# A two-layer attention and MLP kernel: value products on four column tiles, TensorE repack of late outputs, additions shared with GpSimd

## Chip, cores, metric

One core of one Trainium2 chip. The metric is the device time of one launch in microseconds; lower is better. Before: 1644.31 us, median of 3 runs (1643.47 to 1644.97).

## The reference, cut to what matters

Sequence 2048, width 512, two identical layers, each an attention part (A) and a gated MLP part (B):

```python
def _A_ref(x, wq, wk, wv, wo):            # H = 32 heads of 16, one shared K and V head
    q = (x @ wq) -> heads; k = x @ wk; v = x @ wv
    p = softmax(einsum("bhqd,bkd->bhqk", q, k) * 16 ** -0.5)
    return concat_heads(p @ v) @ wo
def _B_ref(x, w1, w2, w3, w4):
    h = gelu(layernorm(x) @ w1); hs = shift_rows(h) @ w2      # rows shifted by 1, -1, 2, -2
    x1 = x + hs
    return x1 + gelu(layernorm(x1) @ w3) @ w4
x = x + A(ln(x)); x = x + B(ln(x)); x = x + A(ln(x)); x = x + B(ln(x))
```

The scores make 32 x 2048 x 2048 exponentials a layer. That is the bulk of the work.

## The kernel before

The program is written by a planner that runs when the kernel is built: every operation is declared with its inputs, an assumed duration and a priority; the planner simulates the engines, decides in which order each engine issues its instructions, and that order is then fixed. Engines work strictly in that order and wait on semaphores.

Attention is cut into 2048 **half-groups** of two heads by 512 scores. Most take the ScalarE way: one exponential of 128 x 1024 values, then one product with V. The others take the VectorE way: two conversions to integers J that read as bf16 powers of two, two additions JK of constants, and three products with V scaled by three weights.

```python
# one half-group on VectorE (cut)
for i in range(2):                                   # two J from PSUM
    o = op("DVE", ... tensor_scalar(J[i], in0=PB[bank], 128*LOG2E*0.25, 127*128, mult, add) ...)
for k in (1, 2):                                     # two JK, from J
    self.adds = [p for p in self.adds if not p.placed]
    eng = "POOL" if len(self.adds) < self.ADDS else "DVE"          # ADDS = 0: always VectorE
    x = op(eng, ... tensor_scalar(JK[r], in0=J, STEPS[k], 1.0, add, mult) ...)

# product with V: head h owns column tile h; half-group p owns two of the four tiles (cut)
for i in range(2):
    h = 2 * p + i
    e.matmul(PB[32*h:32*h+32, ACC, 0:w], lhsT=v[:, la, kb+j, :], rhs=ap[:, i, j*w:(j+1)*w],
             tile_position=(0, 32*h), ...)

# end of a block of four heads: normalise, then move 16 rows a head into OT (cut)
op("SP", lambda e: [e.dma_start(OT[r0+16*h : r0+16*h+16, b//2, 0:n], OS[32*h : 32*h+16, m, 0:n])
                    for h in range(4)], parts=4, prio=5)
```

TensorE also runs fillers, products of zeros that the planner puts in so that TensorE's clock isn't lowered. The MLP of one chunk runs beside the attention of the next. Between the layers lies a **passage**: layer 2 can start on the first tiles, but most of its keys need the end of layer 1. After the last exponential comes the **tail**: what is left of the MLP.

The softmax here doesn't subtract the row's maximum and nothing guards it: scores larger than these inputs give would overflow.

## Time and profile before

| | before |
|---|---|
| time, median (range) | 1644.31 us (1643.47 to 1644.97) |
| span of the profiled run | 1641.6 us |
| ScalarE busy / idle | 1535.7 / 105.9 us |
| exponentials on ScalarE | 1545 of 2048 half-groups |
| ScalarE idle, 770 to 950 us | 29.0 us |
| from the last exponential to the end | 59.0 us |

A busy share alone does not tell whether a shorter busy part would shorten the span. The lines are in the prediction. Two stretches of the time-ordered view of before, start and duration first (us): a value product that stands alone, and the end of the last attention block.

```profile
801.60 0.39 PE L1075 MATMUL PB<-JK,VD 128*32 128x512 bf16 x2
...
1593.51 0.41 DVE L1135 TENSOR_TENSOR OS<-ACCF,PB 128x256 bf16<-128x256 bf16 x1
1593.95 2.41 SPq L1140 DMA_DIRECT2D OT<-OS  x4
...
1597.60 1.91 PE L607 MATMUL PB<-WO,OT 128*32 128x512 bf16 x32 [1.07 <-DMA OT<-OS]
```

Two matmuls, two of four column tiles, where a run of four takes no longer.

### The profile page before, as it was taken

To read this page: it belongs to the slowest core of one execution; us is meant where nothing else is said; L and a number is where in the kernel's file an instruction comes from. 1 tells how busy PE (TensorE), PEld (TensorE's weight loads), DVE (VectorE), ACT (ScalarE), POOL (GpSimd) and SP (SyncE) were. 2 spreads that over 40 slices of the span, in tenths; PEclk is the share of its full clock that TensorE was granted. 3 is DMA by queue.
4 is the path that set the end of the run, shared out by engine and by line. 5 is a ranking of instruction groups with operands and counts; after the bars stand their busy time and mean duration, and the time that the engine had idled before them with its cause. 6 is when DMAs were issued, how large, how long until landed. Compare 5 with 4: busy or idle time off the path is not lost.

```text
span 1641.6 us, 47631 instructions
## 1 busy us (share of the span) xinstructions
PE 1617.8 (99%) x21141; PEld 545.5 (33%) x21141; DVE 1414.8 (86%) x2978; ACT 1535.7 (94%) x1623; POOL 105.6 (6%) x162
## 2 busy tenths in 40 slices
PE   8999999999999999999999999999999999999999
PEld 3222223322332223233333332333223223444454
DVE  8999999889999789898986798998899987899853
ACT  4999999999999999999797999999999999999952
POOL 3000000000010001100120000010000000010001
PEclk9999999999999999999999999999999999999999
DMA  6000000000100000100000000000000000000000
GB/s 204 17 4 4 5 18 5 5 3 5 18 5 3 5 3 5 18 5 5 2 2 2 2 8 8 5 18 4 14 11 4 4 5 11 19 5 5 6 17 18
DMA packets 24398, 20.79 MB, mean 13 GB/s; under 512 B 7168, under 2 KB 23680, under 8 KB 24192
## 3 DMA queue, kind: packets, MB, share of 16 engines
q1 hardware_dynamic: 24192, 17.75, 4.1%
q8 instruction: 165, 2.70, 0.7%
q14 instruction: 41, 0.34, 0.1%
HBM read 7.90 MB, written 2.10 MB: 6 GB/s over the span
## 4 chain that ended last, share of the span: by engine, by line
ACT 75%; PE 22%; DVE 2%; DMA 0%; POOL 0%; issue 0%; SPq 0%; POOLq 0%
ACT EA L997 70%; PE PB L607 10%; PE PB L953 6%; PE PB L1075 5%; ACT G L1364 2%; ACT L997 1%; ACT GP L1288 1%; ACT L1288 1%; PE PB L773 1%; ACT L1364 0%; DVE ST L713 0%; DVE G L1357 0%; DVE ZR L756 0%; DMA X<-in_A_x_dram 0%; POOL X L1371 0%; DVE J L1018 0%
## 5 line engine op out<-in xcount | busy, mean ns | idle before, releaser
L997 ACT ACTIVATE EA<-PB 128x1024 bf16<-128x1024 f32 x1545 | 1423.2, 1084 | 58.4 <-PE PB L1075 34.1
L1018 DVE TENSOR_SCALAR J<-PB 128x512 uint16<-128x512 f32 x1006 | 651.0, 683 | 107.5 <-PE PB L953 103.4
L953 PE MATMUL PB<-QT,KT 32*128 32x512 bf16 (+1 forms) x4608 | 623.3, 360 | 9.9 <-ACT EA L997 7.1
L1075 PE MATMUL PB<-EA,VP 128*32 128x512 bf16 (+1 forms) x3482 | 465.6, 362 | 0.9 <-DVE ACCF L1107 0.3
L1028 DVE TENSOR_SCALAR JK<-J 128x1024 uint16<-128x1024 uint16 x1006 | 387.5, 427 | 13.6 <-PE PB L1075 7.6
L953 PEld LDWEIGHTS PB<-QT,KT 32*128 32x128 bf16 x4608 | 159.9, 91 | 565.8 <-ACT EA L997 506.0
L1075 PE MATMUL PB<-JK,VD 128*32 128x512 bf16 (+1 forms) x2252 | 331.8, 361 | 0.2
L1075 PE MATMUL PB<-J,VD 128*32 128x512 bf16 (+1 forms) x1126 | 186.4, 361 | 2.6 <-DVE J L1018 2.6
L607 PE MATMUL PB<-ZT,W 128*32 128x512 bf16 (+2 forms) x2816 | 170.8, 344 | 0.5 <-DVE J L1018 0.4
L1075 PEld LDWEIGHTS PB<-EA,VP 128*32 128x32 bf16 x3482 | 121.3, 94 | 137.7 <-issue 114.6
L607 PE MATMUL PB<-ONES,NIL 128*32 128x512 bf16 x1416 | 143.7, 392 | 4.5 <-DVE ZR L756 1.3
L1075 PEld LDWEIGHTS PB<-JK,VD 128*32 128x32 bf16 x2252 | 90.5, 95 | 107.2 <-issue 54.7
L607 PE MATMUL PB<-W,G 128*32 128x512 bf16 x1792 | 125.2, 382 | 0.3 <-ACT G L1353 0.2
L730 POOL TENSOR_SCALAR SM<-MV 128x4 f32<-128x4 f32 (+3 forms) x30 | 9.6, 319 | 1137.6 <-DVE MV L715 1137.6
L1357 DVE CAST G<-PB 128x512 bf16<-128x512 f32 (+2 forms) x126 | 72.9, 582 | 10.1 <-PE PB L607 8.5
L607 PEld LDWEIGHTS PB<-ZT,W 128*32 128x32 bf16 x2816 | 57.4, 96 | 56.0 <-issue 33.4
L1075 PEld LDWEIGHTS PB<-J,VD 128*32 128x32 bf16 x1126 | 51.0, 95 | 36.1 <-issue 20.1
L1135 DVE TENSOR_TENSOR OS<-ACCF,PB 128x512 bf16<-128x512 bf16 (+1 forms) x72 | 44.7, 621 | 12.6 <-PE PB L1129 8.1
L1364 ACT ACTIVATE G<-G 128x3584 bf16<-128x3584 bf16 (+2 forms) x18 | 46.0, 2601 | 9.8 <-DVE G L1357 9.7
L607 PEld LDWEIGHTS PB<-W,G 128*32 128x32 bf16 x1792 | 37.5, 95 | 46.9 <-issue 26.8
L607 PEld LDWEIGHTS PB<-ONES,NIL 128*32 128x32 bf16 x1416 | 36.0, 96 | 38.5 <-issue 8.0
L1371 POOL TENSOR_TENSOR X<-Y,X 128x512 f32<-128x512 bf16 x32 | 38.4, 1204 | 154.4 <-DVE Y L1326 149.6
(83 smaller groups left out, 824.5 us busy)
## 6 DMA issues: line engine op xcount, KB each, us to landing
W<-in_B_w_dram SPq DMA_DIRECT2D x2, 1792.0 KB, 15.2
OT<-OS SPq DMA_DIRECT2D x224, 16.0 KB, 1.8
QT<-QS SPq DMA_DIRECT2D x40, 64.0 KB, 2.4
X<-in_A_x_dram SPq DMA_DIRECT2D x8, 256.0 KB, 5.2
out_dram<-OUTB SPq DMA_DIRECT2D x16, 128.0 KB, 1.7
W<-in_B_w_dram SPq DMA_DIRECT2D x2, 512.0 KB, 9.0
OT<-OS SPq DMA_DIRECT2D x64, 8.0 KB, 1.8
WQ<-in_A_wq_dram SPq DMA_DIRECT2D x1, 512.0 KB, 4.9
```

The lines of the kernel that those rows point to most:

```text
L607: ins = e.matmul(self.PB[32 * g:32 * g + 32, bank, 0:n], lhsT=lhsT[:, 32 * g:32 * g + 32], rhs=rhs, start=start, stop=stop, tile_position= ...
L773: ins = e.transpose(self.PBH[:, L.bank, j * 512 + i * 128:j * 512 + (i + 1) * 128], self.ZR[:, tb % 4, dc * 128:(dc + 1) * 128], self.IDENT)
L953: ins = e.matmul(self.PB[:, bank, j * n:(j + 1) * n], lhsT=self.KT[32 * h:32 * h + 32, la, (kb + j) * 128:(kb + j + 1) * 128], rhs=self.QT ...
L997: o = q.feeds = op("ACT", lambda e: e.activation(self.EA[:, ea, :, :], self.PB[:, b0:b0 + 2, :], ACTF.Exp, scale=0.25), writes=bk + [("EA" ...
L1018: o = op("DVE", lambda e, i=i, L=L: e.tensor_scalar(out=J[:, i * 512:(i + 1) * 512], in0=self.PB[:, L.bank, :], scalar1=128 * LOG2E * 0.25 ...
L1028: x = op(eng, lambda e, k=k, r=r: e.tensor_scalar(out=self.JK[:, r, :], in0=J, scalar1=float(self.STEPS[k]), scalar2=1.0, op0=ALU.add, op1 ...
L1075: ins = e.matmul(self.PB[32 * h:32 * h + 32, self.ACC, 0:w], lhsT=v[:, la, kb + j, :], rhs=ap[:, i, j * w:(j + 1) * w], start=first and j ...
L1135: op("DVE", lambda e: e.tensor_tensor(out=self.OS[:, m, 0:n], in0=acc, in1=self.PB[:, M.bank, 0:n], op=ALU.mult), reads=[("ACCF", m)], wri ...
L1288: op("ACT", lambda e: e.activation(self.GP[:, par, :, 2:2 + n], self.GP[:, par, :, 2:2 + n], ACTF.Gelu_apprx_tanh), reads=gt, writes=gt, d ...
L1357: op("DVE", lambda e, f=f, L=L: e.tensor_copy(self.G2[:, f, 0:n], self.PB[:, L.bank, 0:n]), writes=[L, ("G2", f)], dur=t_ps(n), give=L)
L1364: ins = e.activation(self.G2[:, a:a + 7, 0:n], self.G2[:, a:a + 7, 0:n], ACTF.Gelu_apprx_tanh)
L1371: op("POOL", lambda e, tb=tb: e.tensor_tensor(out=self.X32[:, tb, :], in0=self.Y[:, tb % 6, :], in1=self.X32[:, tb, :], op=ALU.add), reads ...
```

## The change

Its intent: use all four column tiles for every product by splitting the columns of each head in two; since the rows of a head then lie in two tiles, moving them to OT takes eight DMAs instead of four, so the planner is given a longer delay for them, and the late blocks of a layer are moved by a selection product on TensorE instead; give up to four outstanding JK additions to GpSimd; shorten the LayerNorm chain on GpSimd; re-tune the planner's constants and some of its rules. Each step of the last MLP product now waits only for the two gelu outputs that it reads, where before it waited for all of them.

```diff
-    EARLY = (7, 11)
+    EARLY = (6, 11)
-    ADDS = 0
+    ADDS = 4
+    LATE_OT = 4
-    BACKLOG = 6
+    BACKLOG = 1
     ... CREDIT, CAP, PATIENCE, SLACK, NEAR_FILL, URGE, LONELY changed, DMA_LATE = 2.5 added; rules for
     ... bunching products rewritten (cut)
@@ product with V
-                for i in range(2):
-                    h = 2 * p + i
-                    ins = e.matmul(self.PB[32 * h:32 * h + 32, self.ACC, 0:w], lhsT=v[:, la, kb + j, :],
-                                   rhs=ap[:, i, j * w:(j + 1) * w], ... tile_position=(0, 32 * h))
+                for x in range(4):
+                    i, u = divmod(x, 2)
+                    ins = e.matmul(self.PB[32 * x:32 * x + 32, self.ACC, p * hw:p * hw + hw], lhsT=v[:, la, kb + j, :],
+                                   rhs=ap[:, i, j * w + u * hw:j * w + u * hw + hw], ... tile_position=(0, 32 * x))
@@ outputs
+        if c == len(self.CHUNKS[la]) - 1 and b >= self.LATE_OT:
+            ... four matmuls with the selection matrix SELO into PSUM, one VectorE copy into OT (cut)
+        else:
             op("SP", lambda e: [ ... for p in range(2) for i in range(2) for u in range(2)],
-               dma=128 * n, parts=4, prio=5)
+               dma=128 * n, parts=8, prio=5)
@@ LayerNorm: the small additions and products go from GpSimd to VectorE, one pow for both roots (cut)
@@ last MLP product
-                op("PE", fpe, reads=g2 + [("W4",)], ...)
+                op("PE", fpe, reads=g2[2 * h:2 * h + 2] + [("W4",)], ...)
```

More of the change, by code (lines that the diff above doesn't have):

```diff
@@ L47 @@
     KEEP = 0.55
-    CREDIT = 0.15
+    CREDIT = 0.2
     URGENT = 0.6
     FORCE = 0.6
-    CAP = 0.5
+    CAP = 0.65
     WAITING = 16.0
@@ L55 @@
     ALONE = 11
-    PATIENCE = 2.0
-    SLACK = 0
-    NEAR_FILL = 0.2
+    PATIENCE = 3.0
+    SLACK = -0.1
+    DMA_LATE = 2.5
+    NEAR_FILL = 0
     STICK = -1
     CLOSE = 0
+    SPARE = 0
     def __init__(self, nc, pool_banks):
@@ L90, in __init__ @@
         self.attach = None
+        self.loose = False
     def op(self, eng, emit, reads=(), writes=(), dur=0.1, prio=None, take=None, give=None,
@@ L152, in _after @@
         lat = self.LAT[o.eng]
+        if p.parts > 1:
+            lat += self.DMA_LATE
         if o.eng == "PE" and o.side:
@@ L225, in _pick @@
                         k = i
-                if k is None:
+                if k is None or o.prio > 2 and len(self.pool) <= self.SPARE and self.attach is not None and not self.loose:
                     continue
@@ L244, in deferred @@
         low = {}
-        ps = [o for o in h if o.pe[0] == "P" and o.prio == 2 and o.ready <= t + 1e-9]
-        if ps and not any(o.ready < t - self.PATIENCE for o in ps):
-            n = [sum(1 for o in ps if o.pe[3][0] == x) for x in (0, 2)]
-            if joins:
-                far = [o for o in ps if self.run_end(o, t) > self.pe_end + 0.06]
-                if 0 in n:
-                    low = {o: self.WAITING for o in far}
-            elif min(n) < (1 if self.pe_kind == "P" else self.BUNCH):
+        if self.pe_kind != "P":
+            ps = [o for o in h if o.pe[0] == "P" and o.prio == 2 and o.ready <= t + 1e-9]
+            if len(ps) < self.BUNCH and not any(o.ready < t - self.PATIENCE for o in ps):
                 low = {o: self.WAITING for o in ps}
@@ L499 @@
               ((0, 4), (4, 4), (8, 4), (12, 2), (14, 2)))
-    EARLY = (7, 11)
-    URGE = ((10, 10, 10, 1.5), (10, 10, 10, 10, 10))
+    EARLY = (6, 11)
+    URGE = ((10, 10, 10, 1.0), (10, 10, 10, 1.5, 10))
     SPILLED = 7
@@ L510 @@
     STEPS = (0, 43, 85)
-    ADDS = 0
-    LN_ENG = "DVE"
+    ADDS = 4
     PARTS = (0.3203125, 0.25390625, 0.2021484375)
@@ L515 @@
     HOLD = 0.1
+    LATE_OT = 4
+    QUICK = -1
     PACE = ((2.8, 2.8, 2.2, 0.3), (2.8, 2.2, 0.5, 0.5, None))
@@ L518 @@
     MAX_PAIRS = 2
-    BACKLOG = 6
+    BACKLOG = 1
     FAR = 20
     FREE = 2
-    LONELY = 4
+    LONELY = 3
     def __init__(self, nc, ins, out):
@@ L557, in memory @@
         self.SELC = sb("SELC", [4])
+        self.SELO = sb("SELO", [2, 32])
         self.WQ = sb("WQ", [4, 528])
@@ L586, in memory @@
         self.MV = sb("MV", [16, 2], dt.float32)
-        self.SM = sb("SM", [6, 16], dt.float32)
-        self.MH = sb("MH", [16], dt.float32)
+        self.SM = sb("SM", [4, 16], dt.float32)
+        self.MH = sb("MH", [2, 16], dt.float32)
         assert self.sbytes <= 208 * 1024, self.sbytes / 1024
@@ L700, in head @@
            reads=[("SELC",)], writes=[("SELC",)], dur=0.2, prio=3)
+        for i in range(2):
+            for u in range(2):
+                op("POOL", lambda e, i=i, u=u: e.tensor_copy(
+                    self.SELO[:, u, 16 * i:16 * i + 16], self.IDENT[:, 32 * (2 * i + u):32 * (2 * i + u) + 16]),
+                    reads=[("ID",)], writes=[("SELO", i, u)], dur=0.1, prio=3)
         fill("POOL", self.GP[:, 0, :, 0:2], 0.0, [("GPL", 0)], 0.1, 3)
@@ L721, in rstd @@
         mv = self.MV[:, a:b, 1]
-        n = b - a
-        s0, s1, s2, s3, s4, s5 = (self.SM[:, i, a:b] for i in range(6))
-        mh = self.MH[:, 0:n]
+        k = 2 if both else 1
         def tg(name):
             return [(name, t) for t in tiles]
-        def root(dst, src, tmp, rd, wr, tw):
-            op("POOL", lambda e: e.tensor_scalar(out=tmp, in0=src, scalar1=EPS, scalar2=None, op0=ALU.add),
-               reads=rd, writes=tw, dur=0.4, prio=prio)
-            op("POOL", lambda e: e.tensor_tensor(out=dst, in0=tmp, in1=mh, op=ALU.pow),
-               reads=tw + [("MH",)], writes=wr, dur=0.3 + 0.2 * n, prio=prio)
@@ L734, in rstd @@
-        root(s0, mv, s4, tg("MV"), tg("R1"), tg("S4"))
-        if self.LN_ENG == "POOL":
-            mean = self.MV[:, a:b, 0]
-            op("POOL", lambda e: e.tensor_tensor(out=s5, in0=s0, in1=mean, op=ALU.mult),
-               reads=tg("R1") + tg("MV"), writes=tg("NM"), dur=0.25, prio=prio)
-            op("POOL", lambda e: e.tensor_scalar(out=s5, in0=s5, scalar1=-1.0, scalar2=0.0, op0=ALU.mult, op1=ALU.add),
-               reads=tg("NM"), writes=tg("NM"), dur=0.25, prio=prio)
-        if both:
-            op("POOL", lambda e: e.tensor_tensor(out=s1, in0=s0, in1=s0, op=ALU.mult),
-               reads=tg("R1"), writes=tg("S1"), dur=0.25, prio=prio)
-            op("POOL", lambda e: e.tensor_tensor(out=s2, in0=s1, in1=mv, op=ALU.mult),
-               reads=tg("S1") + tg("MV"), writes=tg("S2"), dur=0.3, prio=prio)
-            root(s3, s2, s4, tg("S2"), tg("R2"), tg("S4"))
@@ L748, in apply @@
-    def apply(self, out, src, tb, tags, writes, dur, prio):
-        if self.LN_ENG == "POOL":
-            self.pl.op("POOL", lambda e: e.tensor_scalar(
-                out=out, in0=src, scalar1=self.SM[:, 0, tb:tb + 1], scalar2=self.SM[:, 5, tb:tb + 1],
-                op0=ALU.mult, op1=ALU.add),
-                reads=tags + [("R1", tb), ("NM", tb)], writes=writes, dur=0.52, prio=prio, port=True)
-        else:
-            self.pl.op("DVE", lambda e: e.tensor_scalar(
-                out=out, in0=src, scalar1=self.MV[:, tb, 0:1], scalar2=self.SM[:, 0, tb:tb + 1],
-                op0=ALU.subtract, op1=ALU.mult),
-                reads=tags + [("MV", tb), ("R1", tb)], writes=writes, dur=dur, prio=prio, port=True)
+        var, aux = self.SM[:, 2, a:b], self.SM[:, 3, a:b]
@@ new lines, in rstd @@
+        op("DVE", lambda e: e.tensor_scalar(out=var, in0=mv, scalar1=EPS, scalar2=None, op0=ALU.add),
+           reads=tg("MV"), writes=tg("S2"), dur=0.08, prio=prio, port=True)
+        if both:
+            op("DVE", lambda e: e.reciprocal(aux, var), reads=tg("S2"), writes=tg("S3"), dur=0.1, prio=prio)
+            op("DVE", lambda e: e.tensor_tensor(out=aux, in0=aux, in1=mv, op=ALU.mult),
+               reads=tg("MV"), writes=tg("S3"), dur=0.08, prio=prio, port=True)
+            op("DVE", lambda e: e.tensor_scalar(out=aux, in0=aux, scalar1=EPS, scalar2=None, op0=ALU.add),
+               writes=tg("S3"), dur=0.08, prio=prio, port=True)
@@ new lines, in rstd @@
+        op("POOL", lambda e: e.tensor_tensor(out=self.SM[:, 0:k, a:b], in0=self.SM[:, 2:2 + k, a:b],
+                                             in1=self.MH[:, 0:k, a:b], op=ALU.pow),
+           reads=tg("S2") + (tg("S3") if both else []) + [("MH",)], writes=tg("R1") + (tg("R2") if both else []),
+           dur=0.3 + 0.2 * (b - a) * k, prio=self.QUICK if prio is None else prio)
+    def apply(self, out, src, tb, tags, writes, dur, prio):
+        self.pl.op("DVE", lambda e: e.tensor_scalar(
+            out=out, in0=src, scalar1=self.MV[:, tb, 0:1], scalar2=self.SM[:, 0, tb:tb + 1],
+            op0=ALU.subtract, op1=ALU.mult),
+            reads=tags + [("MV", tb), ("R1", tb)], writes=writes, dur=dur, prio=prio, port=True)
@@ L920, in make_groups @@
             if g[5]:
-                self.segs.append(dict(at=g[0:3], end=None, left=0, held=[], open=[False, False]))
+                self.segs.append(dict(at=g[0:3], end=None, left=0, held=[], open=False))
             seg = self.segs[-1]
@@ L998, in declare_unit @@
                                                        scale=0.25),
-                         writes=bk + [("EA", ea)], dur=0.0505 + 1024 / 1200, prio=0, side=False)
+                         writes=bk + [("EA", ea)], dur=0.06 + 1024 / 1200, prio=0, side=False)
         self.units.append(o)
@@ L1045, in add_pv @@
             for g, es in held:
-                if es[0][2] is None or seg["open"][g[5]]:
+                if es[0][2] is None or seg["open"]:
                     for x in es:
@@ L1065, in declare_pv @@
         w = self.size(la, c)
-        first = not seg["open"][p]
-        seg["open"][p] = True
+        hw = w // 2
+        first = not seg["open"]
+        seg["open"] = True
         v, vn = (self.VP, "VP") if part is None else (self.VD[:, part], "VD")
@@ L1072, in fpe @@
             for j in range(nk):
-                for i in range(2):
-                    h = 2 * p + i
-                    ins = e.matmul(self.PB[32 * h:32 * h + 32, self.ACC, 0:w], lhsT=v[:, la, kb + j, :],
-                                   rhs=ap[:, i, j * w:(j + 1) * w], start=first and j == 0, stop=False,
-                                   skip_group_check=True, tile_position=(0, 32 * h))
+                for x in range(4):
+                    i, u = divmod(x, 2)
+                    ins = e.matmul(self.PB[32 * x:32 * x + 32, self.ACC, p * hw:p * hw + hw], lhsT=v[:, la, kb + j, :],
+                                   rhs=ap[:, i, j * w + u * hw:j * w + u * hw + hw], start=first and j == 0,
+                                   stop=False, skip_group_check=True, tile_position=(0, 32 * x))
             return ins
         rd = [(vn, la, kb + j) for j in range(nk)] + (tags if isinstance(tags, list) else [tags])
-        op("PE", fpe, reads=rd + ([] if first else [("AC", p)]), writes=[("AC", p)] if first else [],
-           pe=("P", 512, 256, (2 * p, 2 * p + 1)), prio=2, side=False)
+        op("PE", fpe, reads=rd + ([] if first else [("AC",)]), writes=[("AC",)] if first else [],
+           pe=("P", 256, 256, range(4)), prio=2, side=False)
     def block_end(self, la, c, b, end):
@@ L1088, in block_end @@
                                                                  op=ALU.add),
-                                writes=[("AC", 0), ("AC", 1)] + tags, dur=t_ps(512), prio=0, side=False)
+                                writes=[("AC",)] + tags, dur=t_ps(512), prio=0, side=False)
             return
@@ L1092, in block_end @@
             ap, tags = self.SPILL[b]
-            self.last_copy = op("DVE", lambda e: e.tensor_copy(ap, self.PB[:, self.ACC, :]), writes=[("AC", 0), ("AC", 1)] + tags,
+            self.last_copy = op("DVE", lambda e: e.tensor_copy(ap, self.PB[:, self.ACC, :]), writes=[("AC",)] + tags,
                dur=t_ps(512), prio=0, side=False)
@@ L1104, in block_end @@
                 out=acc, in0=self.PB[:, self.ACC, :], in1=ap, op=ALU.add),
-               reads=tags, writes=[("AC", 0), ("AC", 1), ("ACCF", m)], dur=t_ps(512), prio=0, side=False)
+               reads=tags, writes=[("AC",), ("ACCF", m)], dur=t_ps(512), prio=0, side=False)
         else:
             self.last_copy = op("DVE", lambda e: e.tensor_copy(acc, self.PB[:, self.ACC, 0:n]),
-               writes=[("AC", 0), ("AC", 1), ("ACCF", m)], dur=t_ps(n), prio=0, side=False)
+               writes=[("AC",), ("ACCF", m)], dur=t_ps(n), prio=0, side=False)
         L = Late()
@@ L1138, in block_end, with fo @@
         r0 = 64 * (b % 2)
-        op("SP", lambda e: [
-            e.dma_start(self.OT[r0 + 16 * h:r0 + 16 * h + 16, b // 2, 0:n], self.OS[32 * h:32 * h + 16, m, 0:n])
-            for h in range(4)], reads=[("OS", m)], writes=[("OT", b)], dma=128 * n, parts=4, prio=5)
+        hw = n // 2
+        if c == len(self.CHUNKS[la]) - 1 and b >= self.LATE_OT:
+            N = Late()
+            def fo(e):
+                ins = None
+                for u in range(2):
+                    for p in range(2):
+                        x = r0 + 32 * p
+                        ins = e.matmul(self.PB[x:x + 32, N.bank, u * hw:u * hw + hw], lhsT=self.SELO[:, u, :],
+                                       rhs=self.OS[:, m, p * hw:p * hw + hw], start=True, stop=True,
+                                       tile_position=(0, x), skip_group_check=True)
+                return ins
+            op("PE", fo, reads=[("OS", m)] + [("SELO", i, u) for i in range(2) for u in range(2)], writes=[N],
+               pe=("P", 2 * hw, hw, (r0 // 32, r0 // 32 + 1)), prio=5, take=N)
+            op("DVE", lambda e: e.tensor_copy(self.OT[r0:r0 + 64, b // 2, 0:n], self.PB[r0:r0 + 64, N.bank, 0:n]),
+               writes=[N, ("OT", b)], dur=t_ps(n), prio=5, give=N)
+        else:
+            op("SP", lambda e: [
+                e.dma_start(self.OT[r0 + 16 * (2 * p + i):r0 + 16 * (2 * p + i) + 16, b // 2, u * hw:u * hw + hw],
+                            self.OS[32 * (2 * i + u):32 * (2 * i + u) + 16, m, p * hw:p * hw + hw])
+                for p in range(2) for i in range(2) for u in range(2)],
+               reads=[("OS", m)], writes=[("OT", b)], dma=128 * n, parts=8, prio=5)
         if end == "add" and b >= 3:
@@ L1168, in pump @@
                 and all(o.placed for o in self.units[-2:]) and self.last_copy.placed:
-            self.main_done = True
+            self.main_done = self.pl.loose = True
             for k, o in enumerate(self.units[-2:]):
@@ L1256, in mixer_in @@
             self.apply(self.Y[:, tb % 6, :], self.X32[:, tb, :], tb, [("X", tb)], [("Y", tb % 6)], 0.456, None)
-            op(self.LN_ENG, lambda e, tb=tb: e.tensor_scalar(
-                out=self.ZR[:, tb % 4, :], in0=self.Y[:, tb % 6, :], scalar1=self.SM[:, 3, tb:tb + 1],
+            op("DVE", lambda e, tb=tb: e.tensor_scalar(
+                out=self.ZR[:, tb % 4, :], in0=self.Y[:, tb % 6, :], scalar1=self.SM[:, 1, tb:tb + 1],
                 scalar2=0.0, op0=ALU.mult, op1=ALU.add),
                reads=[("Y", tb % 6), ("R2", tb)], writes=[("ZR", tb % 4)],
-               dur=0.52 if self.LN_ENG == "POOL" else 0.265, port=True)
+               dur=0.265, port=True)
         zs = self.zslot()
@@ L1380, in fpe @@
                     return ins
-                op("PE", fpe, reads=g2 + [("W4",)], writes=[L], pe=tiled(512, 2), take=L if h == 0 else None)
+                op("PE", fpe, reads=g2[2 * h:2 * h + 2] + [("W4",)], writes=[L], pe=tiled(512, 2), take=L if h == 0 else None)
             if la == 0:
```

## The prediction

> **What bounds the kernel now.** I read in this order: the busy shares, the waits of ScalarE, the groups by shape, the chain that ended last, and busy time by stretch.
>
> ```profile
> PE 1617.8 (99%) x21141; PEld 545.5 (33%) x21141; DVE 1414.8 (86%) x2978; ACT 1535.7 (94%) x1623; POOL 105.6 (6%) x162
> ...
> ACT 75%; PE 22%; DVE 2%; DMA 0%; POOL 0%; issue 0%; SPq 0%; POOLq 0%
> ```
>
> TensorE's 99% is not a bound by itself: it includes 1416 filler matmuls of zeros (ONES,NIL), there to keep its clock up, and TensorE ends are modelled. ScalarE owns 75% of the chain. By stretch (columns: length, then PE, PEld, DVE, ACT, POOL busy with counts, clock, DMA):
>
> ```profile
> 40.00:770.00 730.00, 724.99 (x8372) 215.46 (x8368) 657.86 (x1358) 729.35 (x778) 31.48 (x47) 1.00 0.04 7
> 770.00:930.00 160.00, 155.70 (x2144) 57.25 (x2138) 126.15 (x278) 130.99 (x130) 16.53 (x25) 1.00 0.01 2
> 930.00:1540.00 610.00, 604.54 (x8282) 206.69 (x8284) 542.67 (x1137) 609.44 (x647) 31.48 (x46) 1.00 0.03 8
> 1540.00:1642.00 102.00, 97.23 (x1894) 51.19 (x1884) 53.77 (x117) 50.33 (x56) 10.96 (x19) 1.00 0.05 15
> ```
>
> From 40 to 770 us and from 930 to 1540 us ScalarE is busy all the time; what shortens those 1340 us is only fewer exponentials on it. It waits in three places: the head, the passage from layer 1 to layer 2 (770 to 930), and the tail, where TensorE holds it up:
>
> ```profile
> ACT EA L997 <- PE PB L1075: 34.1, 11, 9.6
> ACT EA L997 <- PE PB L953: 23.8, 6, 17.6
> ACT G L1353 <- PE PB L607: 12.9, 14, 10.8
> ACT GP L1280 <- PE PB L607: 10.8, 1, 10.8
> ACT G L1364 <- DVE G L1357: 9.7, 1, 9.7
> ```
>
> Taken stretch by stretch these are 24.5 us of idle in the head, 28.7 in the passage, 1.8 in the second plateau, and 38.5 in the tail plus 12.5 after ScalarE's last instruction: 106 us, and 1535.7 + 106 is the span of 1641.6. So the equation I work with is **span = ScalarE busy + its idle by stage**; the timed median lies 2.7 us above the span.
>
> The work of attention is 2048 half-groups (two heads by 512 scores). 1545 go through an exponential on ScalarE; 503 take another way: two conversions (J) and two additions (JK) on VectorE.
>
> ```profile
> L997 ACT ACTIVATE EA<-PB 128x1024 bf16<-128x1024 f32 x1545 | 1423.2, 1084 | 58.4 <-PE PB L1075 34.1 <-PE PB L953 23.8
> L1018 DVE TENSOR_SCALAR J<-PB 128x512 uint16<-128x512 f32 x1006 | 651.0, 683 | 107.5 <-PE PB L953 103.4
> L1028 DVE TENSOR_SCALAR JK<-J 128x1024 uint16<-128x1024 uint16 x1006 | 387.5, 427 | 13.6 <-PE PB L1075 7.6
> L660 POOL MEMSET QT<- 128x4096 bf16 x1 | 3.5, 3511 | 0.0
> L730 POOL TENSOR_SCALAR SM<-MV 128x1 f32<-128x1 f32 x3 | 0.7, 229 | 140.4 <-DVE MV L715 140.4
> ```
>
> Busy over count, not the mean of one (neighbours overlap), is the price: 0.921 us an exponential, 0.647 a J, 0.385 a JK. A half-group costs VectorE 2 x 0.647 + 2 x 0.385 = 2.06 us, and VectorE, 90% busy on the plateaus, can hardly take more.
>
> **What the Trainium skill says.** (1) "GPSIMD Engine Reference", Engine selection: a one-input elementwise operation is roughly line-rate on GpSimd; section 3.1 gives 1.03 cycles per element at 1.2 GHz for small bodies. The memset here agrees: 3511 ns for 4096 elements, 0.86 ns each. No such addition ran on GpSimd before. (2) "SBUF — State Buffer", Who interferes with whom: VectorE in a two-port mode and GpSimd exclude each other for a whole instruction, while a VectorE instruction with one SBUF input outside these modes is free. The trace agrees: at 277.33 us a run of two JK takes 1.72 us instead of the usual 0.76, and a GpSimd addition of 1.28 us started at 277.49; a J, read from PSUM, beside a GpSimd instruction keeps its length. (3) "TensorEngine Tiling (Array Packing)", Key Properties: tiles work in parallel, and a change of tiling mode drains the array. Here four column tiles of 512 columns end together (4 filler matmuls within 0.40 us, where one alone lasts 0.39). (4) "TensorE: Matmul & The Clock Gate", Part 1: the clock is halved when a window of about 3.4 us is too idle; the clock column stays at 1.00 before, so no loss there today.
>
> **The change, part by part.** Counts of the changed kernel come from its instruction order, which was built but not run.
>
> Value products: two column tiles by 512 columns become four by 256. A half-group's product that stands alone takes 256/2400 = 0.107 us of array time instead of 0.213; a pair that shared the array gains nothing. Matmuls of this kind go from 6,860 to 14,120. TensorE does not set the plateaus, so this saves nothing directly; it lets the products of more VectorE half-groups fit in.
>
> Shared additions: 964 of 1090 JK go to GpSimd. Price of one, an estimate from the skill's 1.03 cycles and the 229 ns of a one-element TENSOR_SCALAR: 1024 x 1.03/1200 + 0.23 = 1.1 us. GpSimd: 964 x 1.1 = 1060, plus 38.4 of residual additions and some 40 of small things: about 1140 us, 71%. VectorE: 1414.8 - 880 x 0.385 + 84 x 0.647 = about 1130, plus perhaps 50 of waiting for the port. Neither becomes the bound.
>
> What reaches ScalarE: its order holds 1503 exponentials and 32 table loads instead of 34. 42 x 0.921 + 2 x 1.28 = 41.3 us less: **busy 1494.4**. So freeing a quarter of VectorE's work buys only 42 half-groups; the rest becomes slack.
>
> Idle by stage afterwards. Head: the same operations, 24. Passage: the last stretch before layer 1 ends holds 34 exponentials instead of 54 between its gelus, the one before 64 instead of 44, so the 9.6 us hole at 787 should largely close while the later ones stay: 19, a choice of mine. Plateaus: 1.8 and an allowance of 6 for late GpSimd results. Tail: after the last score product, TensorE's real work rises from 45.7 to 56.6 us of streaming and fillers fall from 9.6 to 6.0, +7.3; a 6.3 us pair of gelus that lay before the last exponentials moves in and takes the place of idle, -6.3; the output repack by TensorE (two rounds and a VectorE copy of 0.41) replaces a DMA that took 1.8 us to land and ended TensorE's wait at 1597.6, -1: 51. Sum 24 + 19 + 8 + 51 = 102.
>
> The remaining DMA outputs double in number and halve in size; they are 1.8 us each off the chain. The smaller LayerNorm chain on GpSimd saves tenths of a microsecond. Both I take as zero.
>
> **Predicted:** 1494.4 + 102 = 1596.4, plus 2.7: **1599 us**, 2.8% less.
>
> **Rivals.** (a) GpSimd results come late. 933 waits of TensorE in the new order are for GpSimd, and TensorE works in order, so a late JK stops the next score product too. For it: port exclusion, and that 1.1 us is not measured. Against: 29% slack, and VectorE's J does not use the port. If 0.1 us of every third wait reaches ScalarE: +31, 1630. If one addition costs 1.7 us, GpSimd alone needs 964 x 1.7 = 1639 and nothing is gained.
> (b) TensorE becomes the bound through instruction count. In the last two chunks the products have 128 columns, 53 ns of array time for four, while 16 such weight loads at 800.54 us follow each other at 22 ns, 88 for four. The gain of packing is then lost there, though not more than lost: before, a lone pair took 0.107 us per step as well. Against a bound: fillers rise from 354 to 499 groups, so the plan sees more spare time, not less. Worst case about +25: 1624.
> (c) The tail takes it back: if TensorE's added 10.9 us all lie on the chain, +6: 1605.
> (d) Better than I say: the easier TensorE closes all the passage and the allowance is not needed: 1599 - 19 - 6 = 1574, the floor.
>
> **Range and chances.** The certain term is 41.3 us; 2% is 32.9, so only about 8 us may be lost before the verdict is "within 2%", but the passage gives back some 10 in my sum. (a) and (b) make the upper side longer. Range 1577 to 1631; faster 0.70, same 0.24, slower 0.06.
>
> **What would show it.** ScalarE busy near 1494 with 1503 exponentials at 0.92; a GpSimd JK near 1.1 us and GpSimd near 70%; VectorE near 70%; ScalarE's waits on the plateaus below 10 us in all; the passage's idle near 19; the stretch after the last exponential near 66 us. The prediction is wrong if the GpSimd price is above 1.4, if the clock column falls below 1.00, or if ScalarE shows hundreds of short waits for score products.

## The result

1620.63 us median of 4 runs (1618.49 to 1622.03), against 1644.3. The ratio is 0.9855 (95% interval 0.9838 to 0.9872): 1.45% less, within 2%. A ratio is the mean time of one kernel's runs over that of the other's of the same rounds, so not quite the ratio of the medians quoted. The span of the profiled run is 1618.8 us.

The page of the changed kernel, busy time by engine, the two JK groups, and the exponentials:

```profile
PE 1569.8 (97%) x29013; PEld 657.6 (41%) x29013; DVE 1262.5 (78%) x2247; ACT 1501.2 (93%) x1579; POOL 1102.5 (68%) x1064
ACT 64%; PE 31%; DVE 3%; issue 0%; DMA 0%; POOL 0%; SPq 0%; POOLq 0%
L990 ACT ACTIVATE EA<-PB 128x1024 bf16<-128x1024 f32 x1503 | 1391.3, 1096 | 51.5 <-PE PB L946 34.3
L1021 POOL TENSOR_SCALAR JK<-J 128x1024 uint16<-128x1024 uint16 x964 | 1018.9, 1057 | 414.9 <-DVE J L1011 271.5
L1021 DVE TENSOR_SCALAR JK<-J 128x1024 uint16<-128x1024 uint16 x126 | 86.5, 694 | 4.3 <-PE PB L1069 3.3
```

GpSimd took the additions at 1.057 us each and is 68% busy; VectorE went from 86% to 78%. ScalarE's busy time fell by 34.5 us, the span only by 22.8: the rest came back as idle. TensorE's share of the chain rose from 22% to 31%. The busy table by stretch (columns as in the prediction) and ScalarE's waits:

```profile
40.00:770.00 730.00, 710.32 (x12108) 279.38 (x12100) 584.04 (x1002) 727.77 (x769) 557.86 (x532) 1.00 0.04 8
770.00:930.00 160.00, 152.97 (x2656) 65.58 (x2655) 119.42 (x234) 127.14 (x129) 69.21 (x67) 0.99 0.01 2
930.00:1540.00 610.00, 597.82 (x12124) 256.26 (x12112) 485.59 (x836) 601.77 (x634) 444.09 (x425) 1.00 0.04 9
```

```profile
ACT EA L990 <- PE PB L946: 34.3, 14, 18.4
ACT G L1378 <- DVE G L1371: 25.7, 4, 9.3
ACT EA L990 <- PE PB L1069: 16.6, 13, 6.5
ACT GP L1294 <- PE PB L609: 15.8, 1, 15.8
```

The plateaus stayed full (ScalarE busy 727.8 of 730, 601.8 of 610). From 770 to 930 us ScalarE idles 160 - 127.1 = 32.9 us, more than the 29.0 before. The tail takes 71.2 us instead of 59.0; a pair of gelus of 6.3 us has moved into it. In the time-ordered view of the passage, TensorE's MLP products stand in the chain where ScalarE's gelu waits for them:

```profile
862.66 8.59 PE PB L609 x208
871.28 0.57 DVE G L1371
871.87 4.78 ACT G L1378 x2
```

208 MLP matmuls in one run, with no exponential to do beside them: ScalarE waits 8.5 us for this gelu. The repack itself worked: from the end of the last OS at 1555.95 to the output projection at 1556.90 is 0.95 us, where before it was 3.7.

```profile
1555.16 0.79 DVE L1129 TENSOR_TENSOR OS<-ACCF,PB 128x256 bf16<-128x256 bf16 x2
...
1555.97 0.88 DVE L1148 CAST OT<-PB 64x256 bf16<-64x256 f32 x2
...
1556.90 1.91 PE L609 MATMUL PB<-WO,OT 128*32 128x512 bf16 x32
```

### The profile page after: what moved, and what is told of

It reads as the page before. It is cut to its first block, busy times and chain, and to the rows that moved or that the text cites. A ratio compares the mean times of both kernels' runs of the same rounds, so it can differ in the third digit from the quotient of the medians.

```text
span 1618.8 us, 63894 instructions
## 1 busy us (share of the span) xinstructions
PE 1569.8 (97%) x29013; PEld 657.6 (41%) x29013; DVE 1262.5 (78%) x2247; ACT 1501.2 (93%) x1579; POOL 1102.5 (68%) x1064
## 4 chain that ended last, share of the span: by engine, by line
ACT 64%; PE 31%; DVE 3%; issue 0%; DMA 0%; POOL 0%; SPq 0%; POOLq 0%
ACT EA L990 61%; PE PB L609 13%; PE PB L946 9%; PE PB L1069 8%; ACT G L1378 1%; PE PB L766 1%; DVE J L1011 1%; ACT L990 1%; ACT GP L1302 1%; DVE ZR L749 0%; ACT L1302 0%; DMA X<-in_A_x_dram 0%; PE PB L808 0%; DVE ST L720 0%; ACT L1378 0%
## 5 line engine op out<-in xcount | busy, mean ns | idle before, releaser
L990 ACT ACTIVATE EA<-PB 128x1024 bf16<-128x1024 f32 x1503 | 1391.3, 1096 | 51.5 <-PE PB L946 34.3
L1021 POOL TENSOR_SCALAR JK<-J 128x1024 uint16<-128x1024 uint16 x964 | 1018.9, 1057 | 414.9 <-DVE J L1011 271.5
L1011 DVE TENSOR_SCALAR J<-PB 128x512 uint16<-128x512 f32 x1090 | 703.4, 684 | 179.1 <-PE PB L946 174.8
L1069 PE MATMUL PB<-EA,VP 128*32 128x256 bf16 (+1 forms) x6764 | 387.2, 265 | 1.6 <-DVE QT L1081 0.7
L1069 PE MATMUL PB<-JK,VD 128*32 128x256 bf16 (+1 forms) x4904 | 290.1, 265 | 1.6 <-POOL JK L1021 1.2
L1069 PEld LDWEIGHTS PB<-EA,VP 128*32 128x32 bf16 x6764 | 158.5, 95 | 170.5 <-issue 142.7
L609 PE MATMUL PB<-ONES,NIL 128*32 128x512 bf16 x1996 | 178.0, 388 | 9.1 <-DVE ZR L749 3.1
L1069 PE MATMUL PB<-J,VD 128*32 128x256 bf16 (+1 forms) x2452 | 155.2, 263 | 1.3 <-DVE J L1011 0.9
L1021 DVE TENSOR_SCALAR JK<-J 128x1024 uint16<-128x1024 uint16 x126 | 86.5, 694 | 4.3 <-PE PB L1069 3.3
L742 POOL TENSOR_TENSOR SM<-SM,MH 128x4 f32<-128x4 f32 (+4 forms) x30 | 32.0, 1069 | 44.1 <-DVE SM L734 27.8
```

Source lines behind the costliest of these rows:

```text
L609: ins = e.matmul(self.PB[32 * g:32 * g + 32, bank, 0:n], lhsT=lhsT[:, 32 * g:32 * g + 32], rhs=rhs, start=start, stop=stop, tile_position= ...
L742: op("POOL", lambda e: e.tensor_tensor(out=self.SM[:, 0:k, a:b], in0=self.SM[:, 2:2 + k, a:b], in1=self.MH[:, 0:k, a:b], op=ALU.pow), read ...
L990: o = q.feeds = op("ACT", lambda e: e.activation(self.EA[:, ea, :, :], self.PB[:, b0:b0 + 2, :], ACTF.Exp, scale=0.25), writes=bk + [("EA" ...
L1011: o = op("DVE", lambda e, i=i, L=L: e.tensor_scalar(out=J[:, i * 512:(i + 1) * 512], in0=self.PB[:, L.bank, :], scalar1=128 * LOG2E * 0.25 ...
L1021: x = op(eng, lambda e, k=k, r=r: e.tensor_scalar(out=self.JK[:, r, :], in0=J, scalar1=float(self.STEPS[k]), scalar2=1.0, op0=ALU.add, op1 ...
L1069: ins = e.matmul(self.PB[32 * x:32 * x + 32, self.ACC, p * hw:p * hw + hw], lhsT=v[:, la, kb + j, :], rhs=ap[:, i, j * w + u * hw:j * w + ...
```

## The experiments

Since every edit re-plans the whole program, a variant is never the same order with one thing gone. Two controls (e7, e8) were made for that, and a last set (e9 to e12) compares structures after the constants of each were searched again. Idle is the span less ScalarE's busy time; the passage is the idle in the stretch 770 to 950 us; the tail is the time from the end of the last exponential to the end, with the gelus that lie in it. Times are medians; the other columns are from the profiled run.

| kernel | exponentials | time, us | ratio to before | ScalarE busy | idle | passage | tail |
|---|---|---|---|---|---|---|---|
| before | 1545 | 1644.3 | 1 | 1535.7 | 105.9 | 29.0 | 59.0 |
| after | 1503 | 1620.6 | 0.9855 | 1501.2 | 117.6 | 35.1 | 71.2 |
| e1 before + shared adds | 1505 | 1672.4 | 1.0170 | 1496.0 | 177.7 | 61.4 | 85.2 |
| e2 after, no shared adds | 1522 | 1646.8 | 1.0016 | 1518.9 | 124.2 | 35.6 | 70.7 |
| e3 after, DMA outputs | 1506 | 1640.3 | 0.9970 | 1505.4 | 134.0 | 43.9 | 71.8 |
| e4 after, passage adds on VectorE | 1500 | 1623.5 | 0.9873 | 1498.7 | 122.8 | 31.3 | 49.1 |
| e5 less TensorE work | 1500 | 1599.1 | 0.9729 | 1501.0 | 96.0 | 28.4 | 47.9 |
| e6 more to VectorE | 1468 | 1635.3 | 0.9946 | 1466.6 | 169.1 | 51.1 | 83.7 |
| e7 control | 1496 | 1628.5 | 0.9905 | 1499.7 | 127.0 | 38.3 | 58.1 |
| e8 control | 1505 | 1642.0 | 0.9987 | 1506.6 | 131.3 | 43.7 | 63.5 |
| e9 before, retuned | 1520 | 1635.5 | 0.9944 | 1509.9 | 126.1 | 38.1 | 67.9 |
| e10 shared adds, retuned | 1503 | 1640.4 | 0.9976 | 1498.4 | 139.5 | 48.7 | 66.7 |
| e11 packing, retuned | 1497 | 1628.4 | 0.9900 | 1499.5 | 127.7 | 40.8 | 66.9 |
| e12 after, retuned | 1525 | 1619.6 | 0.9849 | 1521.1 | 97.4 | 25.0 | 66.1 |

### e1: the kernel before with shared additions only

```diff
-    ADDS = 0
+    ADDS = 4
```

> The kernel before with only the shared additions switched on (up to 4 outstanding on GpSimd), two-column-tile products kept. Its order holds 1505 exponentials (before 1545, after 1503) and 967 additions on GpSimd. Theory A (the number of exponentials decides, 0.92 us each; packing the products only lets the plan fit more in): about 1644 - 40 x 0.92 = 1607 plus the idle the changed kernel also gained, 1620 in all, so 1605 to 1625. Rival B (without the packing TensorE is too full, the in-order queue falls behind and ScalarE gets gaps on the plateaus): 1640 or more, with tens of us of ScalarE idle on the plateaus.

Measured: 1672.4 us, 1.7% slower than before, with two exponentials more than the changed kernel. Theory A, which was the prediction's, fails: it is 47 us off, more than an order alone was worth in any control (21 us, e8). Rival B gave the sign and part of the place: on the plateaus (40 to 770 and 950 to 1540 us) ScalarE idles 26.6 us, before 1.2. More was lost in the passage (61.4 us idle instead of 29.0), and 14 us after 1540 us.

```profile
ACT EA L997 <- PE PB L953: 65.9, 27, 18.4
ACT G L1364 <- DVE G L1357: 55.0, 4, 26.6
```

55 us of waits before only four gelus, 34 of them after 1540 us: I read this as the MLP lagging behind attention and being left over at the stage ends. So the number of exponentials does not decide by itself.

### e2: the changed kernel without shared additions

```diff
-    ADDS = 4
+    ADDS = 0
```

> The changed kernel with all additions on VectorE again (1522 exponentials, none of the additions on GpSimd). Theory A: 19 exponentials more than after cost 17.5 us, 1638, unless idle changes. Rival B (packing carries the gain, GpSimd brings none and its port lock costs): 1620 or less. Either way VectorE's normalising operations (Y, ZR) go back from 0.59-0.93 us to 0.34-0.54 us if the port lock lengthened them.

Measured: 1646.8 us, 26 slower than after and above both expectations; ScalarE is busy 17.7 us longer (19 exponentials more), the rest is idle. The second expectation holds: VectorE's operations are short again when GpSimd is idle, as the lock on the shared SBUF port would have it. The VectorE groups of e2:

```profile
L1021 DVE TENSOR_SCALAR JK<-J 128x1024 uint16<-128x1024 uint16 x1052 | 396.7, 422 | 10.3 <-PE PB L1069 4.7
L749 DVE TENSOR_SCALAR Y<-X,MV,SM 128x512 bf16<-128x512 f32 x32 | 16.4, 538 | 0.3 <-POOL SM L742 0.3
```

and the same Y in the changed kernel:

```profile
L749 DVE TENSOR_SCALAR Y<-X,MV,SM 128x512 bf16<-128x512 f32 x32 | 28.9, 925 | 6.3 <-POOL SM L742 6.3
```

With GpSimd busy, JK on VectorE goes from 422 to 694 ns and Y from 538 to 925, while a J, read from PSUM, keeps its price (678.8/1052 and 703.4/1090, 0.645 us both). Summed over JK and the normalising groups, the changed kernel's VectorE spends some 75 us more than the prices of before would give.

### e3: all outputs by DMA

```diff
-    LATE_OT = 4
+    LATE_OT = 8
```

> The changed kernel with all outputs by DMA, none repacked by TensorE (1506 exponentials). Theory A: the repack is worth about 1 us at each of the two layer ends plus the 3 exponentials, so 1622 to 1626. Rival (the DMA's landing is on the chain of the passage with its planned delay): 1630 or more, with the passage's idle up by 5 or more.

Measured: 1640.3 us (1634.6 to 1642.6), and 8.8 us more idle in the passage; the rival's numbers. That a landing is on the passage's chain isn't shown: from 700 to 950 us the chain of e3 holds no transfer. In the tail of e3 the delay is in the trace:

```profile
1560.06 23.98 SPq L1152 DMA_DIRECT2D OT<-OS  x32
...
1574.47 0.42 DVE L1129 TENSOR_TENSOR OS<-ACCF,PB 128x256 bf16<-128x256 bf16 x1 [0.84 <-DMA OT<-OS]
...
1585.17 0.61 PE L609 MATMUL PB<-WO,OT 128*32 128x512 bf16 x8
```

The row of 32 joins four blocks of eight DMAs. The queue is idle from 1571.55 to 1573.54 us, until the third block's OS is there; the sixteen of the last two blocks then take 10.5 us, so the last block's OT comes 10.3 us after its OS (1574.89 to 1585.17) instead of 0.95. The repack repairs this delay, which packing made. How much of it reached the end is less clear: TensorE had other MLP products meanwhile, and from the last OS to the end e3 takes 64.5 us, only 1.7 us longer than the changed kernel. Part of the 20 us goes with TensorE's clock: the execution at a mean of 0.999 took 1634.6 us, those at 0.992 to 0.994 took 1639.4 to 1642.6. What of the rest is the DMAs and what the new order, e3 alone can't tell (see e8).

### e4: GpSimd's additions kept out of the passage

```diff
+            passage = self.segs[g[6]]["end"] in ("spill", "more")
-            eng = "POOL" if len(self.adds) < self.ADDS else "DVE"
+            eng = "POOL" if len(self.adds) < self.ADDS and not passage else "DVE"
```

> The changed kernel with the additions of the early and spilled segments of layer 2 (those computed in the passage between the layers) on VectorE, GpSimd free there; 1500 exponentials. Theory P (GpSimd additions hold the shared port and lengthen VectorE's normalising chain in the passage, so ScalarE runs dry for longer): ScalarE idle from 770 to 930 us falls from 33 to under 25 and the time to 1605-1612. Rival S (the passage is set by TensorE's chain of MLP products and by the supply of half-groups, whatever GpSimd does): idle there stays 29 to 36 and the time is 1616 to 1621.

Measured: 1623.5 us; idle from 770 to 950 us is 31.3 instead of 35.1. Theory P predicted under 25; so there is no sign that the port lock of these additions makes the passage long. The time is 2.5 us above S's band, within what the order alone does (below).

### e5: less TensorE work, wrong on purpose

```diff
-            for h in range(7):
+            for h in range(0, 7, 2):
```

> Wrong result on purpose: the changed kernel with 6 of the 14 accumulation steps of the last MLP product left out, 768 matmuls or 41 us of array time, about 15 us of it in the passage and 11 in the tail; 1500 exponentials (after 1503), so ScalarE's own work falls only by 3 us. Theory T (in the passage and the tail TensorE is the bound, ScalarE runs dry because of it): ScalarE idle from 770 to 950 us and after the last exponential falls, 20 to 26 us in all, time 1592 to 1600. Rival L (these stretches are set by latencies of LayerNorm, outputs and gelu): idle there falls by under 8 us, time 1610 to 1618.

Measured: 1599.1 us. ScalarE's busy time is that of after (1501.0); its idle fell by 21.6: by 6.7 in the passage (35.1 to 28.4) and 17.1 after the last exponential (from 51.8 to 34.7, the tail less the gelus and table load in it), while 2.2 came back elsewhere. The rows of both (columns as in the prediction); in the passage ScalarE was busy 144.9 us of 180 in the changed kernel:

```profile
770.00:950.00 180.00, 171.62 (x2927) 72.79 (x2925) 138.09 (x274) 151.62 (x157) 95.18 (x91) 0.98 0.01 3
1540.00:1597.00 57.00, 52.43 (x1190) 28.37 (x1186) 26.50 (x61) 17.07 (x26) 8.85 (x11) 1.00 0.07 23
1540.00:1619.00 79.00, 73.46 (x1648) 40.93 (x1640) 38.21 (x87) 26.50 (x31) 13.97 (x16) 1.00 0.05 18
```

The first two are e5's, the third is the changed kernel's. So taking work from TensorE alone, at the same ScalarE load, shortens the kernel by what theory T says, to 20 us below the fastest order of the full work that was run (e12). The split is not T's, which put 15 us in the passage and 11 in the tail. From 1540 us on ScalarE idles 39.9 us, in the orders of the full work (after, e4, e7, e8, e12) 44.8 to 52.3; in the passage e5's 28.4 lies among their 25.0 to 43.7. So that TensorE holds up the whole and the tail is shown, that it holds up the passage is not. (The output still passed the tolerance, which says something of the tolerance and nothing of the time.)

### e6: more half-groups to VectorE

```diff
-    FREE = 2
+    FREE = 1
```

> The changed kernel with VectorE allowed a new half-group when one PSUM bank of the pool is free instead of two: 1468 exponentials, 35 fewer than after, and 70 more product steps on TensorE. Theory A (exponentials decide): 35 x 0.92 = 32 us less, 1588. Theory T (TensorE is the second bound, what is not done beside the plateaus is done in the passage and the tail): most of it returns as ScalarE idle at the stage ends, time 1610 to 1630.

Measured: 1635.3 us: 35 exponentials fewer than after and 15 us **slower**. Theory A said 1588; the 47 us between are more than the controls below (8 and 21 us), the 15 us over the changed kernel are not.

```profile
ACT EA L990 <- PE PB L946: 57.4, 20, 17.9
ACT EA L990 <- PE PB L1069: 44.4, 20, 7.6
ACT G L1378 <- DVE G L1371: 37.1, 3, 27.2
```

ScalarE's busy time is 34.6 us below that of after, its idle 51.5 above. Of the 51, 25 lie on the plateaus (33.2 instead of 8.2), 16 in the passage and 12 after 1540 us; 1 was won in the head. A half-group moved to VectorE costs TensorE two more product steps. My reading, which fits these waits but is not shown: on the plateau they now delay score products, and TensorE does less of the MLP beside them, which is still there at the stage end, when there are no exponentials to hide it.

### e7 and e8: controls

```diff
-    CREDIT = 0.2
+    CREDIT = 0.21
```

> A control: one constant of the build-time planner moved by a hair (0.20 to 0.21), no operation added or taken away, but the order comes out different (1496 exponentials). If the order alone matters little, 1614 to 1624; if the luck of the order is as large as the differences seen so far (3 to 20 us), outside of that.

```diff
-    DMA_LATE = 2.5
+    DMA_LATE = 2.6
```

> A second control: the planned delay of the split DMAs 2.6 us instead of 2.5, the same operations in another order (1505 exponentials). As for the first control: 1616 to 1627 if the order alone matters little.

Measured: 1628.5 and 1642.0 us (two runs each), both outside the bands for an order that matters little. The operations are those of the changed kernel; only the planner's choices differ, and the time is 8 and 21 us longer. e8's profiled run had the same mean clock as that of after (0.998) and took 1639.7, so it isn't the clock. So the order alone can be worth nearly as much as the whole change, and e2 to e4 and e6 can't be read as the worth of one part. What can be read from them are the waits and durations that their traces show directly.

### e9 to e12: structures compared after a search of constants

For each structure some 500 settings of the planner's constants were drawn (505, 512 and 553) and the one that the planner itself reckons best was built; for the changed kernel some 5800, so its search was not the same. The edits are constants only, for e12:

```diff
-    CAP = 0.65
+    CAP = 0.55
-    EARLY = (6, 11)
-    URGE = ((10, 10, 10, 1.0), (10, 10, 10, 1.5, 10))
+    EARLY = (7, 11)
+    URGE = ((10, 10, 10, 1.5), (10, 10, 10, 1.5, 10))
-    HOLD = 0.1
+    HOLD = 0.15
-    LONELY = 3
+    LONELY = 4
```

(e9 changes CREDIT, PATIENCE, BACKLOG, LONELY, FAR, HOLD, URGE and PACE of the kernel before; e10 and e11 the like, with ADDS = 4 on before and ADDS = 0 on after.)

> The operations of the kernel before, with only constants of its build-time planner changed: the best of 505 drawn settings by the planner's own reckoning (1520 exponentials, 272 filler groups). The three kernels that differ from the changed one by a hair or little (1620.6, 1628.5, 1642) say that the order alone is worth up to 21 us. Theory O (a good part of the change's 24 us is a better order, not new operations): 1628 to 1638. Rival N (the new operations are needed for it): 1640 to 1650.

> The kernel before with shared additions only (two-column-tile products, four DMAs), best of 512 settings drawn in the same way; 1503 exponentials. Under theory T (TensorE has no room for more product steps at 0.213 us each) it is no better than the retuned kernel before: 1630 to 1645. If shared additions alone carry the gain: 1615 to 1625.

> The changed kernel without shared additions (four-column-tile products, TensorE repack, new LayerNorm chain), best of 553 settings drawn in the same way; 1497 exponentials. Under theory T packing is what gives TensorE room: faster than both the retuned kernel before and the retuned shared additions, 1618 to 1630. Rival: no faster than the retuned kernel before.

> The changed kernel's operations with the best of some 5800 settings: 1525 exponentials, 22 more than after. If exponentials decided: 1641. If what counts is how much of TensorE's work fits beside them before the stage ends: 1610 to 1624, in spite of 20 us more on ScalarE, with correspondingly less ScalarE idle in the passage and the tail. It is also the attempt at a version that beats both.

Measured: 1635.5, 1640.4, 1628.4 and 1619.6 us, each within the band of theory O or T. In steps: better constants on the old operations give 9 us; shared additions without packing give nothing on top (5 us slower than e9); packing with the repack, the new LayerNorm chain, the finer waits and the new planner rules gives 7 us over e9; shared additions on top of packing another 8 to 9. Each step compares two orders, and none is larger than what one control moved (21 us), so the steps are suggested and not shown. Part goes with the clock too: e9's executions at a mean of 0.998 and 0.999 took 1633.2 and 1631.8 us, the two at 0.994 took 1637.8; e11's ran at 0.988 to 0.995. e12 is the clearest case of the sum. Two lines of its page:

```profile
PE 1563.4 (97%) x28905; PEld 647.8 (40%) x28905; DVE 1198.0 (74%) x2137; ACT 1521.1 (94%) x1601; POOL 1122.4 (69%) x1086
L990 ACT ACTIVATE EA<-PB 128x1024 bf16<-128x1024 f32 x1525 | 1411.2, 1098 | 45.2 <-PE PB L946 22.5
```

22 exponentials more than after, 19.9 us more ScalarE busy time, 20.2 us less idle, and the same time. It is no real gain over the changed kernel (1 us, within the spread), so the search found no version that clearly beats both.

## Why the prediction was right or wrong

The measured time lies in the stated range, 21 us above the number, and "within 2%" had been given 0.24 against 0.70 for faster. Step by step:

- **ScalarE is full on the plateaus, GpSimd and VectorE do not become the bound: right.** The plateaus show 2.2 and 8.2 us of idle in 730 and 610. An addition on GpSimd took 1.057 us (estimate 1.1) and GpSimd was 68% busy (71%). Rival (a) did not happen: all waits of TensorE for a GpSimd result sum to 1.2 us. VectorE came out at 78% instead of about 73%: operations lengthened beside GpSimd cost 75 us instead of 50, some 23 us of small LayerNorm operations and OT copies were left out, and the records of neighbours overlap 33 us less (VectorE's groups sum to 108.6 us more than its busy time before, to 75.2 after).
- **"busy 1494.4": 6.8 us short.** The count was exact, the price was not: an exponential came to 1391.3/1503 = 0.926 us instead of 0.921. My reading, argued and not shown: exponentials in a row overlap by some 0.15 us in the record (one at 879.36 us of e9 is 1.06 long, a row is 0.92 apart), so a start that is a little late shows as a longer span and not as idle.
- **"Passage: ... 19, a choice of mine": the step that failed.** Over the same stretch it was 32.9. I took the shift of 20 exponentials from the last part of the passage to an earlier one as idle closed. The hole only moved: 8.55 us before 825 us instead of 9.64 before 796, with further ones before two gelus (8.5 and 4.25). This term is 14 of the 22 us between the predicted and the measured span. What the runs show in its place: the passage's idle depends on how the order spreads its work (25.0 to 43.7 us in the table among after, e4, e7, e8 and e12, with nearly equal operations), and the changed kernel has a new wait there, of a gelu behind 208 MLP matmuls (8.5 us). That TensorE's unfinished MLP makes the passage long fits e1, e5 and e6 but is not shown; the cause of these 14 us stays open. (The 28.7 and 1.8 us of idle that the prediction reads for before are 29.0 and 0.6 by its own table.)
- **Tail 51: right in the sum** (52.3 from 1540 us on, 51.8 of it after the last exponential), in part by luck: before holds a wait of 4.9 us before its last exponential, which went, and the stretch after it came out at 71.2 us and not near 66. Head 24: right (22.0). With the repack OT came 2.7 us sooner after OS than before, not 1, and 9.3 us sooner than with eight DMAs (e3), though from OS to the end e3 takes only 1.7 us longer.
- **"42 x 0.921" as the certain term: wrong as a cause,** though the sum was kept. The 42 came; of the 34.5 us that ScalarE was busy less, 11.7 came back as idle. e5 (as many, 22 us faster) shows that the count is one side of a balance with TensorE's work; e12 (22 more than after, as fast) and e6 (35 fewer, 15 us slower) fit it, one order each. Rival (b) looked for TensorE in the number of instructions and dismissed it because of the fillers. Its 1624 is near the result; no run tests its mechanism. Fillers stand for moments with nothing ready, and I took them for room.
- **A sign of being wrong came up, faintly:** the clock column reads 0.99 from 770 to 930 us, before 1.00. The changed kernel's execution at a mean of 1.000 took 1618.5 us, those at 0.998 took 1620.6 to 1622.0, so it is worth some 2 to 4 us here.
- **Not foreseen:** the order itself. A forecast that reads a gain of 2.8% off counts should have carried the 8 to 21 us that a neutral change of order makes here.

What stays open: how much of the last step, from e11 to the changed kernel, is shared additions and how much the better-searched constants or the clock; what the finer waits of the last MLP product gave; and why one order leaves less in the passage than another with equal counts. The counts of fillers and exponentials don't sort the runs.

## What to carry to other kernels

When one engine is full for most of the time, write the span as its busy time plus its idle by stage, and ask of each operation moved off it what the move costs the engine that does the rest in the idle stages. Where a planner or scheduler sets the order, run a neutral change first: its spread is the error bar of every experiment that takes out one part, and structures are compared only after each has had the same search. A split that makes a layout worse (eight DMAs for four) must be charged with the repair, and the repair judged against the split, not against the kernel before; and a delay that was repaired counts only as far as it reached the end.

## What the Trainium skill lacked or had wrong

- "Perfetto Trace Analysis", Identifying the Most-Contended Engine, calls occupancy of ScalarE a fair measure of how close a kernel is to roofline. That isn't refuted here, but it did not tell which work to cut: 93% (after) and 94% (e12) took the same time, 94% (before) was 24 us slower, and 34.6 us less work on ScalarE made e6 15 us slower than after.
- "SBUF — State Buffer", Who interferes with whom: the traces agree with the exclusive lock. It gives no price for a mixed stream; here a JK went from 0.42 to 0.69 us on average with GpSimd 68% busy, and VectorE took some 75 us longer in all.
- "GPSIMD Engine Reference", Engine selection, "roughly line-rate" for one input, holds for a 16-bit addition too: 1.057 us for 1024 elements per partition. The page has no figure for that type.
- "DMA: Bandwidth & Descriptors", Rules for kernel authors, advises to merge many small transfers into one; packing went the other way. The page has no time measured on this chip for issuing one. Four took 2.41 us in SyncE's queue, 0.60 us each, while each lands about 2 us after its issue. The queue of sixteen (10.5 us), more than the landing, delayed OT by 10.3 us in e3.
- No page warns that a planner's order is a variable: 8 and 21 us (0.5% and 1.3%) from a hair's change in one constant (e7, e8).
